# A table of steps for the output rows of one half batch: turns six steps later, ranks one step later

## The chip, the cores and the metric

The kernel runs on one core of one Trainium2 chip. The metric is the time of one execution on the device in microseconds (us), from the first to the last instruction with what lies around them. A core has engines that run at once and wait for each other through semaphores: TensorE (PE in the rows; PEld is its weight load), VectorE (DVE), ScalarE (ACT), GpSimd (POOL) and SyncE (SP), which here only issues DMA transfers.

## The reference

Three stages run one after another on 8 batches with 8 heads of 576 rows, 4608 rows of 512 numbers in all. Cut to what is computed:

```
a      = softmax(phi)                       # over 32 memory slots
k_m    = a^T k ;  v_m = a^T v               # per head, 32 x 64
x      = softmax(q k_m^T / 8) v_m           # attention over the slots
h      = x @ w_in                           # 512 -> 2048
g      = where(h > 0, h, exp(min(h, 0)) - 1)
y      = g @ w_out                          # 2048 -> 512
logits = y @ w_gate ;  e = argmax(logits)   # 8 experts
out    = softmax(logits)[e] * relu(y @ w1[e]) @ w2[e]
```

## The kernel before

**Units and steps.** The first two stages work on half batches: a batch b has two groups g of 288 rows. The hidden 2048 columns are cut into 16 pieces f, and a triple (b, g, f) is one unit. The list `seq` puts the units in order; the first batch is cut, so that pieces 0 to 7 of its group 1 come first, then all of its group 0 (units 8 to 23), then pieces 8 to 15 of group 1 (units 24 to 31). Units from 32 on are the second batch.

**What a step issues.** From unit 23 on, step i of the program first issues whatever was put on the list `bg` for it, then `mm1` of unit i+2 (six matmuls, L520), `elu` of it (ACT L527 and L528, DVE L529) and `split_g` of it (ACT L536, POOL L537), and last `mm2` of unit i (twelve matmuls, L551). Every engine takes its instructions in the order in which they are issued here: the kernel is written under a manual schedule, and nothing reorders them.

**What lies on the list.** For the batch after the one in hand, `attn_items` puts the pieces of its attention on steps 3 to 25 of a group: `a1` turns phi (DVE L347) and takes its maximum (L349), `a1e` is the exponential (ACT L356), `a2` turns the result back (PE L372, copied out by ACT L373), `a3` multiplies with k and v (PE L380), `a3b` scales and turns (DVE L390 to L399), `a4` makes the scores (PE L424, DVE L429), `a5` takes their maximum (DVE L434). `load_phi` (SP L201) fetches phi for the other half of the heads into the one buffer of its kind, once `a1` has read it. `a6n` folds v_m into w_in (PE L482, evacuated by ACT L491 and DVE L492) and then loads the next piece of w_in (SP L340). PE's small products share two PSUM buffers, `ps_m`.

**What follows a group.** When the last unit of a group is done, its sums stand in `ysb`, and `y_items` puts the rest on the steps behind it: the logits (`y_logit`, `y_logit2`), the ranks (`y_rank`: two matmul lines on PE, L611 and L612, and DVE L620 to L633), three scatters of row numbers (`y_scatter`, POOL L685), four turns of the sums into rows (`y_turn`, DVE L656, into the tile `yr`), the gate weights (`y_gate`, DVE L664 and L668), three multiplications by them (`y_times`, DVE L673), and the store of the rows to DRAM (`y_store`, SP L679, four DMAs of 144 KB). The tile `yr` has one buffer, so a group's first turn waits until the store of the group before it has landed.

For group 0 of the first batch the last step is 23, and its store stands at step 32; for group 1 the last step is 31, and what `y_items` puts for it counts from there. The steps are a table of thirteen numbers, `t`: logits, second logits, ranks, first scatter, four turns, two gate steps, three multiplications (the last of which is also the store's).

Of the kernel before, what the change touches and what calls it, by code (L numbers as in the profile page):

```python
# [57 lines left out]
def attn_moe_moe2_kernel(  # L58
# [112 lines left out]
    with ExitStack() as order:  # L171
        order.enter_context(tc.manual_schedule())
        setup()
        with ExitStack() as p1, ExitStack() as late_pool:
# [394 lines left out]
            def y_logit(b, g):  # L569
                ysb = st["y", b, g]  # L570
                ps = ps_m.tile([P, 512], F32, tag="m", name="ps_l")
                for c in range(NC):
                    nc.tensor.matmul(ps[32 * c:32 * c + 32, 0:G], wg[:, c, :], ysb[c], tile_position=(0, 32 * c))  # L573
                lp = l1.tile([P, G], F32, tag="e", name="lp", bufs=3)
                nc.scalar.copy(out=lp, in_=ps[:, 0:G])
                st["lp", b, g] = lp

            def y_logit2(b, g):
                lp = st.pop(("lp", b, g))
                ps = ps_m.tile([P, 512], F32, tag="m", name="ps_l2")  # L580
                n = G // PK
                for i in range(n):
                    nc.tensor.matmul(ps[:PK, E * i:E * i + E], lp[:, PK * i:PK * i + PK], sel)
                lg = ps[:PK, 0:n * E].rearrange("p (i e) -> p i e", e=E)
                tl = lambda shape, name, dt=F32: pool.tile(shape, dt, tag=name, name=name)
                bc = lambda x: x.to_broadcast([PK, n, E])
                mx = tl([PK, n, 1], "r_mx")
                nc.vector.tensor_reduce(out=mx, in_=lg, axis=AX.X, op=ALU.max)
                sh = tl([PK, n, E], "r_sh")
                nc.vector.tensor_tensor(out=sh, in0=lg, in1=bc(mx), op=ALU.subtract)  # L590
                ex = tl([PK, n, E], "r_ex")
                nc.scalar.activation(out=ex, in_=sh, func=AF.Exp)
                oh = tl([PK, n, E], "r_oh")
                nc.vector.scalar_tensor_tensor(
                    out=oh, in0=sh, scalar=0.0, in1=prio[:PK].unsqueeze(1).to_broadcast([PK, n, E]),
                    op0=ALU.is_ge, op1=ALU.mult,
                )
                nc.vector.tensor_reduce(out=mx, in_=oh, axis=AX.X, op=ALU.max)
                nc.vector.tensor_tensor(out=oh, in0=oh, in1=bc(mx), op=ALU.is_equal)
                gate = pool.tile([PK, n, 1], F32, tag="r_gate", name="r_gate", bufs=2)  # L600
                nc.vector.tensor_reduce(out=gate, in_=ex, axis=AX.X, op=ALU.add)
                nc.vector.tensor_scalar(out=gate, in0=gate, scalar1=1e-9, scalar2=None, op0=ALU.add)
                nc.vector.reciprocal(out=gate, in_=gate)
                st["oh", b, g], st["gate", b, g] = oh, gate

            def y_rank(b, g):
                oh = st.pop(("oh", b, g))
                n = G // PK
                flat_oh = oh.rearrange("p i e -> p (i e)")
                ps = ps_m.tile([P, 512], F32, tag="m", name="ps_r")  # L610
                nc.tensor.matmul(ps[:, 0:n * E], ones, flat_oh)  # L611
                nc.tensor.matmul(ps[:PK, 64:64 + n * E], tri, flat_oh)  # L612
                if b == 0 and g == 0:
                    nc.tensor.matmul(
                        ps[:, 128:128 + E], ident[0:PK, 0:1].to_broadcast([PK, P]), oh[:, 0, :]
                    )
                    nc.vector.tensor_copy(out=oh0, in_=ps[:, 128:128 + E])
                for i in range(n):
                    nxt = run[:, g, i + 1] if i + 1 < n else run[:, 1 - g, 0]
                    nc.vector.tensor_tensor(out=nxt, in0=run[:, g, i], in1=ps[:, E * i:E * i + E], op=ALU.add)  # L620
                rk = pool.tile([PK, n, E], F32, tag="r_sh", name="rk")
                nc.vector.tensor_tensor(
                    out=rk, in0=ps[:PK, 64:64 + n * E].rearrange("p (i e) -> p i e", e=E),
                    in1=run[:PK, g, 0:n], op=ALU.add,
                )
                nc.vector.tensor_tensor(out=rk, in0=rk, in1=oh, op=ALU.mult)
                df = pool.tile([PK, n, 1], F32, tag="r_mx", name="df")
                nc.vector.tensor_reduce(out=df, in_=rk, axis=AX.X, op=ALU.add)
                di = pool.tile([PK, n, 1], I32, tag="r_di", name="di", bufs=2)
                if (b, g) == (B - 1, 1):  # L630
                    st["df"] = df
                else:
                    nc.vector.tensor_copy(out=di, in_=df)  # L633
                st["di", b, g] = di
# [17 lines left out]
            def y_turn(b, g, c):  # L652
                if c == 0:
                    st["yr", b, g] = late["p"].tile([P, NB, NC, 32], F32, tag="yr", name="yr", bufs=1)
                x = st["y", b, g][c].rearrange("p (j s) -> p j s", s=32)
                nc.vector.transpose(out=st["yr", b, g][:, :, c], in_=x)  # L656

            def y_gate(b, g, part):
                gate = st["gate", b, g]
                k = PK // 32  # L660
                if part == 0:
                    g4 = st["g4", b, g] = pool.tile([P, G // PK, k], F32, tag="r_g4", name="r_g4")
                    for x in range(k):
                        nc.vector.tensor_copy(out=g4[0:32, :, x], in_=gate[32 * x:32 * x + 32, :, 0])  # L664
                else:
                    g4 = st["g4", b, g]
                    for x in range(1, 4):
                        nc.vector.tensor_copy(out=g4[32 * x:32 * x + 32], in_=g4[0:32])  # L668

            def y_times(b, g, i, n=NR):  # L670
                yr = st["yr", b, g].rearrange("p j c i -> p j (c i)")[:, n * i:n * i + n]
                g4 = st["g4", b, g].rearrange("p i x -> p (i x)")[:, n * i:n * i + n].unsqueeze(2)
                nc.vector.tensor_tensor(out=yr, in0=yr, in1=g4.to_broadcast([P, n, P]), op=ALU.mult)  # L673

            def y_store(b, g):
                yr = st["yr", b, g].rearrange("p j c i -> p j (c i)")
                rows = table[4 * S * b:4 * S * b + 4 * S, :].rearrange("(s j x) d -> x s j d", j=NJ, x=4)
                for x in range(4):
                    nc.sync.dma_start(out=rows[x, :, NB * g:NB * g + NB], in_=yr[32 * x:32 * x + 32])  # L679
# [3 lines left out]
            def y_scatter(b, g, i):  # L683
                t = (G // PK) * (2 * b + g) + i
                d = nc.gpsimd.indirect_dma_start(  # L685
                    out=itab.rearrange("a (l o) -> (a l) o", o=1),
                    out_offset=IndirectOffsetOnAxis(ap=st["di", b, g][:, i], axis=0),
                    in_=ids[:, t:t + 1], in_offset=None,
                )
                for x in scattered:  # L690
                    tc.declare_no_dep(d.ins, x.ins, reason="a token's place is its own")
                scattered.append(d)
# [80 lines left out]
            def y_items(b, g):  # L773
                t = [1, 2, 7, 8, 4, 4, 9, 9, 11, 13, 15, 16, 17] if g else [1, 2, 9, 10, 4, 5, 9, 11, 11, 12, 12, 13, 13]
                if b == 0 and g == 0:
                    t = [1, 2, 6, 7, 3, 4, 5, 5, 6, 6, 7, 8, 9]
                it = [
                    (t[0], lambda: y_logit(b, g)), (t[1], lambda: y_logit2(b, g)), (t[2], lambda: y_rank(b, g)),
                ]
                it += [(t[3] + i, lambda i=i: y_scatter(b, g, i)) for i in range(G // PK)]  # L780
                it += [(t[4 + c], lambda c=c: y_turn(b, g, c)) for c in range(NC)]
                it += [(t[8 + i], lambda i=i: y_gate(b, g, i)) for i in range(2)]
                it += [(t[10 + i], lambda i=i: y_times(b, g, i)) for i in range(NB // NR)]
                it += [(t[12], lambda: y_store(b, g))]
                if b == 0 and g == 0:
                    it += [(11, y_first)]
                return it
# [72 lines left out]
            for i, (b, g, f) in enumerate(seq):  # L860
# [20 lines left out]
                if f == NF - 1:  # L881
                    for s, fn in y_items(b, g):
                        at(i + s, fn)
# [524 lines left out]
```

## Time and profile before

| what | value |
|---|---|
| median of 3 runs | 1283.53 us (1281.06 to 1286.11) |
| the profiled execution's own time | 1290.46 us |
| its span, first to last instruction | 1288.7 us |
| PE busy | 1207.3 us, 94% of the span |
| DVE, ACT, POOL busy | 62%, 52%, 36% |
| mean granted clock of TensorE | 0.979 of full |
| the chain that ended last, by engine | PE 75%, DMA 8%, DVE 7% of the span |
| the store `table<-yr` in that chain | 1% of the span |

The profile is of one execution. It lists each instruction with its start from the beginning of the span, its duration, and how long its engine sat idle before it with the instruction or transfer that ended the idle time. "The chain that ended last" follows the work back from its last instruction, at each step to what released it. The granted clock is 1.00 at 2.4 GHz and 0.50 at 1.2 GHz.

### The profile page before, as it was taken

To read this page: it belongs to the slowest core of one execution; us is meant where nothing else is said; L and a number is where in the kernel's file an instruction comes from. 1 tells how busy PE (TensorE), PEld (TensorE's weight loads), DVE (VectorE), ACT (ScalarE), POOL (GpSimd) and SP (SyncE) were. 2 spreads that over 40 slices of the span, in tenths; PEclk is the share of its full clock that TensorE was granted. 3 is DMA by queue.
4 is the path that set the end of the run, shared out by engine and by line. 5 is a ranking of instruction groups with operands and counts; after the bars stand their busy time and mean duration, and the time that the engine had idled before them with its cause. 6 is when DMAs were issued, how large, how long until landed. Compare 5 with 4: busy or idle time off the path is not lost.

```text
span 1288.7 us, 26251 instructions
## 1 busy us (share of the span) xinstructions
PE 1207.3 (94%) x10026; PEld 1114.4 (86%) x10026; DVE 799.7 (62%) x1811; ACT 665.0 (52%) x1523; POOL 461.6 (36%) x497
## 2 busy tenths in 40 slices
PE   4488886999999999999999999999999999999997
PEld 2277766989989898899899899999999999999995
DVE  5899764655655564655656544673677666667672
ACT  3677543555555565555555555531445444445442
POOL 2656241353443443443444444412222321131102
PEclk9689998999999999999999999999999999999999
DMA  9776656643652544544451252314578777557763
GB/s 232 195 211 193 180 114 125 123 110 77 126 125 51 132 118 55 150 94 93 121 91 42 85 168 57 74 21 121 137 185 259 212 205 241 156 144 194 215 209 95
DMA packets 113786, 178.41 MB, mean 138 GB/s; under 512 B 10745, under 2 KB 79609, under 8 KB 110064
## 3 DMA queue, kind: packets, MB, share of 16 engines
q1 hardware_dynamic: 105632, 157.09, 47.9%
q0 software_dynamic: 8016, 19.52, 5.4%
q8 instruction: 82, 1.34, 0.5%
q14 instruction: 56, 0.46, 0.2%
HBM read 171.62 MB, written 42.76 MB: 166 GB/s over the span
## 4 chain that ended last, share of the span: by engine, by line
PE 75%; DMA 8%; DVE 7%; issue 4%; ACT 3%; POOL 1%; SPq 1%; POOLq 0%; DVEq 0%; ACTq 0%
PE ps_acc L551 27%; PE ps_h L520 15%; PE ps_h L1081 14%; PE ps_acc L1096 12%; DMA kv<-in_v_dram 3%; PE ps_M L482 2%; PE ps_kv L380 2%; DMA out_dram<-xr,idw 1%; DMA table<-yr 1%; PE ps_s L424 1%; DMA win_x<-in_moe_w_in_dram 1%; PE ps_l L573 1%; DVE e L529 1%; PE ps_a L372 1%; DVE gl L537 1%
## 5 line engine op out<-in xcount | busy, mean ns | idle before, releaser
L537 POOL TENSOR_TENSOR gl<-e,gh 128x288 fp32r<-128x288 f32 x237 | 196.3, 828 | 394.0 <-ACT gh L536 306.9
L520 PE MATMUL ps_h<-ath,wt 128*128 128x288 f32 x1024 | 262.6, 313 | 9.2 <-DVE e L529 8.3
L529 DVE SCALAR_TENSOR_TENSOR e<-e,ps_h 128x288 f32<-128x288 f32 x256 | 114.1, 446 | 207.0 <-ACT e L528 189.1
L520 PEld LDWEIGHTS ps_h<-ath,wt 128*128 128x128 f32 x1024 | 182.0, 192 | 54.0 <-issue 30.0
L536 ACT CAST gh<-e 128x288 fp32r<-128x288 f32 x256 | 110.4, 432 | 185.4 <-DVE e L529 183.6
L551 PE MATMUL ps_acc<-gh,wt 128*128 128x288 f32 x1024 | 179.3, 297 | 3.4 <-ACT gh L536 3.3
L551 PE MATMUL ps_acc<-gl,wt 128*128 128x288 f32 x1024 | 178.4, 296 | 1.6 <-DVE gl L537 1.6
L551 PE MATMUL ps_acc<-gh,wl 128*128 128x288 f32 x1024 | 178.3, 296 | 0.0
L1084 ACT ACTIVATE hh<-ps_h 128x288 fp32r<-128x288 f32 x128 | 52.6, 411 | 225.7 <-PE ps_h L1081 200.9
L1081 PE MATMUL ps_h<-xh,wt 128*128 128x288 f32 x1024 | 164.8, 300 | 2.2 <-ACT xh L747 1.0
L551 PEld LDWEIGHTS ps_acc<-gh,wt 128*128 128x128 f32 x1024 | 151.3, 190 | 4.7 <-ACT gh L536 4.5
L520 PE MATMUL ps_h<-atl,wt 128*128 128x288 f32 x512 | 152.8, 298 | 0.5 <-POOL atl L470 0.5
L551 PEld LDWEIGHTS ps_acc<-gl,wt 128*128 128x128 f32 x1024 | 151.1, 189 | 2.3 <-DVE gl L537 2.3
L1081 PEld LDWEIGHTS ps_h<-xh,wt 128*128 128x128 f32 x1024 | 144.7, 189 | 8.9 <-ACT xh L747 5.5
L551 PEld LDWEIGHTS ps_acc<-gh,wl 128*128 128x128 f32 x1024 | 150.7, 190 | 0.0
L527 ACT ACTIVATE e<-ps_h 128x288 f32<-128x288 f32 x256 | 104.6, 409 | 59.7 <-PE ps_h L520 49.9
L1085 DVE SCALAR_TENSOR_TENSOR hl<-ps_h,hh 128x288 fp32r<-128x288 f32 x128 | 58.2, 455 | 121.2 <-ACT hh L1084 113.6
L1109 POOL DMA_INDIRECT out_dram<-xr,idw x42 | 42.7, 1016 | 240.3 <-DMA xr<-od 215.7
L528 ACT ACTIVATE e<-e 128x288 f32<-128x288 f32 x256 | 113.9, 445 | 8.1
L520 PEld LDWEIGHTS ps_h<-atl,wt 128*128 128x128 f32 x512 | 99.1, 193 | 0.7 <-POOL atl L470 0.7
L1096 PE MATMUL ps_acc<-hh,wl 128*128 128x288 f32 x576 | 90.8, 299 | 1.3 <-issue 1.3
L1081 PE MATMUL ps_h<-xl,wt 128*128 128x288 f32 x512 | 89.5, 296 | 1.3 <-DVE xl L748 1.3
(214 smaller groups left out, 1924.2 us busy)
## 6 DMA issues: line engine op xcount, KB each, us to landing
raw<-in_moe_w_dram SPq DMA_DIRECT2D x30, 2048.0 KB
win<-win_s SPq DMA_DIRECT2D x28, 1024.0 KB
xd<-xr SPq DMA_DIRECT2D x17, 576.0 KB
xg<-xd SPq DMA_DIRECT2D x68, 144.0 KB
kv<-in_k_dram SPq DMA_DIRECT2D x16, 576.0 KB
kv<-in_v_dram SPq DMA_DIRECT2D x16, 576.0 KB
table<-yr SPq DMA_DIRECT2D x64, 144.0 KB
od<-ot SPq DMA_DIRECT2D x64, 144.0 KB
```

The source lines that it names most:

```text
L520: nc.tensor.matmul(ps, x[:, u, fo:fo + P], y[:, u], start=(n == 0), stop=(n == 3 * NQ - 1))
L527: nc.scalar.activation(out=e, in_=ps, func=AF.Relu, scale=-1.0)
L528: nc.scalar.activation(out=e, in_=e, func=AF.Exp, scale=-1.0)
L529: nc.vector.scalar_tensor_tensor(out=e, in0=e, scalar=-1.0, in1=ps, op0=ALU.add, op1=ALU.max)
L536: nc.scalar.copy(out=gh, in_=e)
L537: eng.tensor_tensor(out=gl, in0=e, in1=gh.bitcast(F32), op=ALU.subtract)
L551: nc.tensor.matmul(acc[c], x[:, f, P * c:P * c + P], y, start=(first and n == 0), stop=(final and n == 2),)
L1081: nc.tensor.matmul(ps, w1_at(p, y, c, f), x[:, c], start=(n == 0), stop=(n == 3 * NC - 1))
L1084: nc.scalar.activation(out=h, in_=ps, func=AF.Relu)
L1085: V.scalar_tensor_tensor(out=l, in0=ps, scalar=0.0, in1=h.bitcast(F32), op0=ALU.max, op1=ALU.subtract)
L1096: nc.tensor.matmul(acc[c], w2t[p][:, y, f, P * c:P * c + P], x, start=(f + n == 0), stop=(f == NF2 - 1 and n == 2),)
L1109: d = nc.gpsimd.indirect_dma_start(out=out, out_offset=IndirectOffsetOnAxis(ap=at(n), axis=0), in_=xp["r"][:, n], in_offset=None, bounds_c ...
```

## The change

One table of steps is split off for group 1 of the first batch. Until now that group used the table of all groups 1.

```diff
                 t = [1, 2, 7, 8, 4, 4, 9, 9, 11, 13, 15, 16, 17] if g else [1, 2, 9, 10, 4, 5, 9, 11, 11, 12, 12, 13, 13]
                 if b == 0 and g == 0:
                     t = [1, 2, 6, 7, 3, 4, 5, 5, 6, 6, 7, 8, 9]
+                elif b == 0:
+                    t = [1, 2, 8, 9, 10, 10, 12, 12, 11, 13, 15, 16, 17]
```

The turns go from steps 35, 35, 40, 40 to 41, 41, 43, 43; the ranks from 38 to 39; the scatters, which count from the fourth number, from 39 to 41 to 40 to 42. Gates, multiplications and store stay.

On DVE at step 35, behind the last vector work of step 34, stand the turns (`yr`) and the turn of phi (`pT`) with its maximum (`nm`):

```order
 L648 SCALAR_TENSOR_TENSOR rowb<-erow,less 128x8 [waits DVE_49]
 L529 SCALAR_TENSOR_TENSOR e<-e,ps_h 128x288 [waits Activation_49]
-L656 STREAM_TRANSPOSE yr<-ysb 128x9x32 [waits DMAHW2_49,DMAHW7_49,DMAHW1_49,DMAHW0_49]
-L656 STREAM_TRANSPOSE yr<-ysb 128x9x32
-L347 STREAM_TRANSPOSE pT<-phi_t 128x576
+L347 STREAM_TRANSPOSE pT<-phi_t 128x576 [waits DMAHW7_49]
 L349 TENSOR_REDUCE nm<-pT 128x1 [waits DVE_49]
```

The first two turns, with their wait for the four DMAs of a store, no longer stand ahead of phi's turn, which has a DMA wait of its own instead.

On PE at steps 38 and 39 stand the products for w_in (`ps_M`), the ranks (`ps_r`), matmuls of units, and `a3` (`ps_kv`):

```order
 L482 MATMUL ps_M<-win,vT 32x512 x8
-L611 MATMUL ps_r<-r_oh,ones 128x24
-L612 MATMUL ps_r<-r_oh,tri 96x24
 L520 MATMUL ps_h<-ath,wt_82 128x288
...
 L551 MATMUL ps_acc_1951<-gl,wt_82 128x288
+L611 MATMUL ps_r<-r_oh,ones 128x24
+L612 MATMUL ps_r<-r_oh,tri 96x24
 L380 MATMUL ps_kv<-kv,a 32x128 x24
```

The two rank matmuls move from directly behind `ps_M` to directly ahead of `ps_kv`, past the 18 matmuls of a step.

On DVE at steps 40 to 43, behind `a3b`, stand the vector part of the units (`e`), the gates (`r_g`), the scores (`sT`) and their maximum (`mx`):

```order
 L399 STREAM_TRANSPOSE kT<-kvm 32x64 x4
-L529 SCALAR_TENSOR_TENSOR e<-e,ps_h 128x288 x2
-L664 COPY r_g_2364<-r_gate 32x3 x3
+L529 SCALAR_TENSOR_TENSOR e<-e,ps_h 128x288
+L656 STREAM_TRANSPOSE yr<-ysb 128x9x32 x2
+L529 SCALAR_TENSOR_TENSOR e<-e,ps_h 128x288
+L664 COPY r_g_2362<-r_gate 32x3 x3
 L429 STREAM_TRANSPOSE sT<-ps_s 128x288 x2
 L529 SCALAR_TENSOR_TENSOR e<-e,ps_h 128x288
+L656 STREAM_TRANSPOSE yr<-ysb 128x9x32 x2
 L434 TENSOR_REDUCE mx<-sT 128x18
```

One pair of turns now stands between the vector work of two units at step 41, the other ahead of the scores' maximum at step 43.

## Rows read from the trace of the kernel before

**Rows 1.** Chain that ended last, 180 to 220 us: start, us, what.
```profile
189.18 15.80 DMA table<-yr
205.17 0.84 DVE yr L656 x2
206.01 0.67 DVE pT L347
208.62 1.52 PE ps_a L372 x6
```

**Rows 2.** Waits on PE, 180 to 260 us: total, times, longest.
```profile
PE ps_a L372 <- ACT aT L356: 8.6, 1, 8.6
PE ps_r L611 <- DVE wt L492: 1.5, 1, 1.5
```

**Rows 3.** Timeline of PE: start, us, instruction, [idle before, releaser].
```profile
199.31 0.69 PE L551 MATMUL ps_acc<-gl,wt 128*128 128x288 f32 x4
...
213.81 1.09 PE L482 MATMUL ps_M<-win,vT 64*32 64x512 f32 x16
216.36 0.40 PE L611 MATMUL ps_r<-r_oh,ones 96*128 96x24 f32 x2 [1.46 <-DVE wt L492]
...
216.77 0.38 PE L520 MATMUL ps_h<-ath,wt 128*128 128x288 f32 x1
...
219.34 1.52 PE L380 MATMUL ps_kv<-kv,a 96*32 96x128 f32 x48
...
225.67 0.82 PE L372 MATMUL ps_a<-ident,aT 128*96 128x128 f32 x6
226.25 0.38 PE L520 MATMUL ps_h<-ath,wt 128*128 128x288 f32 x1
...
228.81 1.20 PE L424 MATMUL ps_s<-big,kT 32*32 32x288 f32 x32
...
238.88 0.29 PE L520 MATMUL ps_h<-ath,wt 128*128 128x288 f32 x1
```

**Rows 4.** Windows: stretch, engines' busy us, granted clock, DMA share, GB/s.
```profile
198.00:200.00 2.00, 2.00 (x16) 1.77 (x14) 0.00 (x0) 0.00 (x0) 0.02 (x1) 1.00 1.05 79
204.00:206.00 2.00, 0.00 (x0) 0.00 (x0) 0.83 (x3) 0.00 (x0) 0.00 (x0) 0.50 0.73 279
210.00:212.00 2.00, 2.00 (x9) 2.00 (x9) 0.75 (x2) 1.38 (x4) 0.81 (x1) 0.50 0.00 0
214.00:216.00 2.00, 0.90 (x16) 0.00 (x0) 0.66 (x2) 1.44 (x3) 0.79 (x1) 1.00 0.01 4
```

**Rows 5.** Timeline of ACT, the steps that follow phi's turn.
```profile
207.49 1.06 ACT L356 ACTIVATE aT<-pT,nm 128x576 f32<-128x576 f32 x1 [10.41 <-DVE nm L349]
...
212.08 0.85 ACT L373 COPY a<-ps_a 96x384 f32<-96x384 f32 x2
```

**Rows 6.** Timeline of DVE, 196 to 237 us.
```profile
196.16 0.45 DVE L529 SCALAR_TENSOR_TENSOR e<-e,ps_h 128x288 f32<-128x288 f32 x1
...
209.44 0.45 DVE L529 SCALAR_TENSOR_TENSOR e<-e,ps_h 128x288 f32<-128x288 f32 x1 [1.99 <-ACT e L528]
...
216.97 0.55 DVE L620 TENSOR_TENSOR run<-run,ps_r 128x8 f32<-128x8 f32 x3
...
218.06 0.17 DVE L633 CAST di<-df 96x3 int32<-96x3 f32 x1
...
219.27 0.77 DVE L347 STREAM_TRANSPOSE pT<-phi_t 128x576 f32<-128x576 f32 x1
...
222.94 0.45 DVE L529 SCALAR_TENSOR_TENSOR e<-e,ps_h 128x288 f32<-128x288 f32 x1 [2.12 <-ACT e L528]
...
228.78 0.46 DVE L529 SCALAR_TENSOR_TENSOR e<-e,ps_h 128x288 f32<-128x288 f32 x1 [2.10 <-ACT e L528]
...
236.89 0.46 DVE L529 SCALAR_TENSOR_TENSOR e<-e,ps_h 128x288 f32<-128x288 f32 x1 [3.40 <-ACT e L528]
```

**Rows 7.** Timeline of SP, the DMAs that it issues.
```profile
184.09 0.34 SPq L340 DMA_DIRECT2D win<-win_s  x1
187.29 2.85 SPq L679 DMA_DIRECT2D table<-yr  x4
192.76 0.34 SPq L340 DMA_DIRECT2D win<-win_s  x1
206.70 0.35 SPq L201 DMA_DIRECT2D phi_t<-in_phi_dram  x1
```

## Prediction

> **What bounds the kernel now.** I read the page first: PE is busy for 94% of the span, and most of the chain that ended last is its matmuls. So only an edit that takes an idle stretch off PE, or adds one, moves the time. Then the waits on PE around the place of the change. From 180 to 260 us there are two of size [rows 2]: 8.6 us before the first `a2` of the second half's work (step 37), and 1.5 us before the ranks (step 38).
>
> The chain says where the 8.6 us come from [rows 1]. The store of group 0's rows takes 15.80 us from its last issue to its landing; only then can DVE begin the turns of group 1 (205.17), which write the same buffer; behind them stand phi's turn (206.01), its maximum, the exponential on ACT (207.49 [rows 5]) and at last PE's `a2` (208.62). DVE had been ready since its vector work of 196.16 plus 0.45 us [rows 6]. The reader is to see that phi's turn needs nothing from that store. It stands behind the turns on an engine that works in order.
>
> The windows show a second price [rows 4]: the granted clock is 1.00 while PE still works (198 to 200 us), 0.50 in the idle stretch and also from 210 to 212 us, when PE is busy again, and 1.00 from 214 us. That is 1.2 GHz in place of 2.4 GHz for the first matmuls after the idle stretch.
>
> **The change part by part.** Times are those of the profiled execution.
>
> The turns out of step 35. Phi's turn can start at 196.61. From there to the exponential is what it was: 207.49 less 206.01, 1.48 us, so ACT starts at 198.09, 9.40 us earlier than before. `a2` came 1.13 us after that start (208.62 less 207.49), so it could begin at 199.22. PE is free at 200.00 (208.62 less 8.62; the last group before it started at 199.31 [rows 3]). So the exponential is ready 0.8 us before PE, and the whole 8.62 us goes.
>
> The clock. From `a2` to the next `ps_M` took 5.19 us at half clock (208.62 to 213.81). The same row of work, six transposes, `mm1` and `mm2`, took 3.14 us later at full clock (225.67 to 228.81 [rows 3]). Without the idle stretch nothing lowers the clock: 2.05 us gained.
>
> What is late next. The chain of ACT and DVE behind the exponential keeps its own pace, shifted by 9.40 us. The unit's vector work of 209.44 ends at 200.49, and `mm1` behind `a2` wants that buffer at 200.58: no wait. The copies of `a2` (212.08, 0.85 us [rows 5]) end at 203.53, and `ps_M` needs the buffers that they free; PE would be there at 200.00 + 3.14 = 203.14. A new wait of 0.39 us.
>
> The ranks. PE waited 1.46 us for the evacuation of `ps_M` [rows 3], since the two small buffers were both taken. Now `mm1` of step 38 follows `ps_M` at once, and the ranks come 18 matmuls later. Those took 2.57 us (216.77 to 219.34), more than the 1.46 us for which the evacuation was late, so it is done by then: 1.46 us gained. Their own 0.41 us on PE (216.36 to 216.77) moves and stays. On DVE they take 1.26 us (216.97 to 218.23), and that now stands ahead of the second phi turn of step 39. The vector work behind it, which ended at 223.39, would end 1.26 us later against PE, and its buffer is wanted at 226.25: 1.6 us of cover are left, so nothing. The scatters go one step later with them on POOL; nothing on PE waits for a scatter.
>
> The turns at their new steps. A pair is 0.84 us. At step 40 a pair goes from ahead of `a3b`, so DVE is 0.8 us sooner there. At step 41 the pair stands where DVE sat idle for 2.10 us waiting for ACT (228.78 [rows 6]); at step 43 ahead of `mx`, where the next unit's vector work had waited 3.40 us for ACT's exponential and ended at 237.35, 1.5 us before the matmul that needs its buffer (238.88). Full delay of 0.84 us is covered. The wait for the store itself: 205 us against about 216 for step 41. Cost nothing; if all cover were gone, 0.84 us for each pair.
>
> Phi's second load. SP issued it at 206.70, at the end of phi's turn, into an idle queue, and no DMA moved after 210 us [rows 4, 7]: at most 3.3 us. Now it is issued at about 197.3, with the store and the load of `win` (192.76) still under way; they keep the DMAs busy until about 206. If it goes behind them, it lands between 206 and 206 + 3.3 = 209.3. It is wanted at 219.27 - 11.74 + 1.26 = 208.8, and PE feels it only after the 1.6 us of cover, from 210.4 on. I take zero, with a loss of up to 4.9 us kept for the range (worked out below). By the Trainium skill (DMA: Bandwidth & Descriptors, "Queues, rings and completion order") each DMA engine takes a queue's descriptors in ring order, which puts this load behind the whole store. The store's landing at 205 and the burst of 279 GB/s that ends by 206 [rows 1, 4] agree with one after another. By that rule the landing is the later one above; with bandwidth shared out, the sooner one; the sum is the same by both.
>
> Sum: 8.62 + 2.05 + 1.46 - 0.39 = 11.74 us. The steps after the place keep their order and their distances, so the gain stays to the end. The profiled execution, 1290.46 us of its own (span 1288.7 us), would be 1278.7; the median of the runs shown, 1283.53, goes to 1271.8.
>
> Bounds: at most 8.62 + 2.05 + 1.46 = 12.1 us if no new wait appears. The other end is set by the rivals.
>
> **The rivals.**
> *Phi's load takes the store's place.* For it: it now enters the queue in a stretch that moved only 79 GB/s at full DMA share [rows 4], and the store took 15.80 us there. Against it: by 204 to 206 us the DMAs moved 279 GB/s again. If a second slow stretch as long as from 198 to 204, 6 us, struck this load, it would land at 209.3 + 6 = 215.3; DVE's second phi turn would wait, and PE would lose 215.3 - 210.4 = 4.9 us. Gain 6.8 us, 1276.7. The ring order that the Trainium skill states (DMA: Bandwidth & Descriptors, "Queues, rings and completion order") is what would put the load into this place.
>
> *The wait is mostly the profiled execution's own.* It took 6.93 us more than the median. If all of that lay in this one wait, plain runs would lose only 8.62 - 6.93 = 1.69 us there, and no clock. The gain is then 1.69 + 1.46 - 0.39 = 2.8 us: 1280.8. Against it: in the page's chain DMAs hold 8% of the span and this store 1%, so a surplus of slow DMAs would lie mostly elsewhere.
>
> *The change does not do what it says.* In the new order phi's turn waits on a DMA semaphore (DMAHW7) that is one of the four for which the turns waited. If that meant the store's second part, the stall would remain and only 1.46 us would go: 1282. Against it: these count up, and phi's first load was issued on it before the store, as its own transfer, so its count is reached long before.
>
> *Slower.* One mechanism: DVE stuck at step 39 on phi's second load for longer than it was at step 35 on the store. Place: the second phi turn; price: each us of landing after 210.4 is a us on PE, with the clock's 2.05 us once it idles long. Break-even is a landing at about 220, slower by 0.5% (6.4 us) at about 226, which is 29 us after issue, where the longest transfer here took 15.80 us. At 230 it would be 1293. Only a queue blocked twice over does that.
>
> **How the numbers follow.** Forecast 1271.8 us at 0.74; phi's load late, 1276.7, at 0.10; the profile's own wait, 1280.8, at 0.11; not as it says, 1282, at 0.02; slower, 1293, at 0.03. The forecast's own range is 1268.5 to 1275: 12.1 us of gain and the runs' spread of 2.5 us below and above the median. For 8 in 10 I go up into the second and third case, to 1279. What a measurement of this kernel can tell from no change is 0.5%, 6.4 us, so faster means under 1277.1: nearly all of the first case (0.73), half of the second (0.05), a fifth of the third (0.02), 0.80 together. Within it 0.17, slower 0.03.
>
> **What would show it.** In the changed profile PE's wait before `a2` at about 200 us is under 1 us, and the granted clock stays at 1.00 from 196 to 216 us; `ps_kv` of step 39 starts near 207.6 in place of 219.34; DVE's turns at about 216 and 220 wait for no DMA; the ranks do not appear among PE's waits. Wrong would be: a wait for phi's load at DVE's second phi turn that reaches PE, a wait for `e` (L529) on PE's `mm1` at steps 43 to 47 above 1 us, or a group of waits elsewhere that has grown by what was won here.

## The result and the profile after

The changed kernel takes 1271.85 us (median of 4 runs, 1269.79 to 1273.14); before, on the same chip, takes 1282.57 us. The ratio is 0.9911, with a 95% interval of 0.9885 to 0.9937. Once more with more rounds it was 1272.22 us beside 1283.77 us, ratio 0.9911 (0.9898 to 0.9924). The forecast was 1271.8 us.

The profiled spans differ by more, 1288.7 to 1271.4 us, and the place of the change does not hold all of that: a second profile of before (below) has a span of 1284.1 us with the same stall in it, so the first one was slow elsewhere too. So I read the place by itself, from the `ps_M` of step 34 to the `ps_kv` of step 39, in both timelines of PE.

The timeline of PE after, the stretch that answers to [rows 3] (start, us, instruction, idle before where there was a wait):

```profile
193.52 1.09 PE L482 MATMUL ps_M<-win,vT 64*32 64x512 f32 x16
...
201.82 0.82 PE L372 MATMUL ps_a<-ident,aT 128*96 128x128 f32 x6
...
205.23 1.46 PE L482 MATMUL ps_M<-win,vT 64*32 64x512 f32 x16
206.62 0.40 PE L520 MATMUL ps_h<-ath,wt 128*128 128x288 f32 x1
...
209.13 0.30 PE L611 MATMUL ps_r<-r_oh,ones 96*128 96x24 f32 x2
...
209.53 1.52 PE L380 MATMUL ps_kv<-kv,a 96*32 96x128 f32 x48
```

No row has an idle time. From 193.52 to 209.53 are 16.01 us. Before, the same stretch began with this row of PE's timeline:

```profile
191.54 1.09 PE L482 MATMUL ps_M<-win,vT 64*32 64x512 f32 x16
```

It ended at 219.34 [rows 3], after 27.80 us: 11.79 us won at the place.

All waits on PE from 180 to 260 us, to be set beside [rows 2]:

```profile
PE ps_acc L551 <- ACT gh L536: 0.6, 1, 0.6
PE ps_h L520 <- POOL atl L470: 0.5, 1, 0.5
PE ps_l L573 <- DVE wt L492: 0.5, 1, 0.5
```

Both waits of before are gone, and none of their size has come. The windows (stretch, engines' busy us, granted clock, DMA share, GB/s), as [rows 4]:

```profile
200.00:202.00 2.00, 2.00 (x17) 2.00 (x17) 0.06 (x1) 1.84 (x4) 0.00 (x0) 1.00 1.27 94
206.00:208.00 2.00, 2.00 (x25) 1.38 (x11) 0.58 (x2) 1.41 (x4) 0.57 (x1) 1.00 0.76 275
214.00:216.00 2.00, 2.00 (x18) 1.99 (x17) 0.92 (x4) 1.38 (x6) 0.07 (x1) 1.00 1.10 234
```

The DMAs are as slow as before (94 GB/s at full share), but PE works through that time, and the clock stays at 1.00. On DVE the turns stand where they were put, and phi's second turn has no wait for its load. DVE's timeline after:

```profile
198.51 0.77 DVE L347 STREAM_TRANSPOSE pT<-phi_t 128x576 f32<-128x576 f32 x1
...
209.63 0.56 DVE L620 TENSOR_TENSOR run<-run,ps_r 128x8 f32<-128x8 f32 x3
...
210.31 0.75 DVE L626 TENSOR_TENSOR rk<-rk,r_oh 96x24 f32<-96x24 f32 x1
...
211.38 0.77 DVE L347 STREAM_TRANSPOSE pT<-phi_t 128x576 f32<-128x576 f32 x1
...
214.94 0.45 DVE L529 SCALAR_TENSOR_TENSOR e<-e,ps_h 128x288 f32<-128x288 f32 x1 [2.00 <-ACT e L528]
...
217.86 0.83 DVE L656 STREAM_TRANSPOSE yr<-ysb 128x288 f32<-128x288 f32 x2
...
223.12 0.83 DVE L656 STREAM_TRANSPOSE yr<-ysb 128x288 f32<-128x288 f32 x2
```

### The profile page after: what moved, and what is told of

Read it like the earlier page. It is cut to its first block, busy times and chain, and to the rows that moved or that the text cites. A ratio compares the mean times of both kernels' runs of the same rounds, so it can differ in the third digit from the quotient of the medians.

```text
span 1271.4 us, 26251 instructions
## 1 busy us (share of the span) xinstructions
PE 1202.2 (95%) x10026; PEld 1110.1 (87%) x10026; DVE 799.4 (63%) x1811; ACT 663.2 (52%) x1523; POOL 461.1 (36%) x497
## 4 chain that ended last, share of the span: by engine, by line
PE 74%; DVE 8%; DMA 7%; issue 4%; ACT 3%; POOL 2%; SPq 1%; POOLq 0%; DVEq 0%; ACTq 0%
PE ps_acc L551 28%; PE ps_h L520 15%; PE ps_h L1083 12%; PE ps_acc L1098 10%; PE ps_M L482 3%; PE ps_kv L380 2%; DMA out_dram<-xr,idw 1%; PE ps_s L424 1%; DVE e L529 1%; DMA kv<-in_v_dram 1%; DMA big<-in_q_dram 1%; DMA xg<-xd 1%; PE ps_l L573 1%; DVE gl L537 1%; DMA win_x<-in_moe_w_in_dram 1%
## 5 line engine op out<-in xcount | busy, mean ns | idle before, releaser
L520 PE MATMUL ps_h<-ath,wt 128*128 128x288 f32 x1024 | 261.0, 311 | 10.7 <-DVE e L529 9.8
```

What stands on the lines that cost most here:

```text
L520: nc.tensor.matmul(ps, x[:, u, fo:fo + P], y[:, u], start=(n == 0), stop=(n == 3 * NQ - 1))
```

## The experiments

My theory: the gain is the wait for the store (8.6 us) with the half clock behind it, and the wait before the ranks; nothing else moved. Rivals: the ranks carry it, DVE's order is a cost in itself, the stall belongs to one execution, or phi's load has little or no cover. The place is told by three distances in PE's timeline: from the `ps_M` of step 34 to `a2`, from there to the `ps_M` of step 38, from there to `ps_kv`.

| kernel | to `a2` | to `ps_M` | to `ps_kv` | together | ratio of time to before (95%) |
|---|---|---|---|---|---|
| before | 17.08 | 5.19 | 5.53 | 27.80 | |
| before again | 16.43 | 5.56 | 5.52 | 27.51 | |
| after | 8.30 | 3.41 | 4.30 | 16.01 | 0.9911 (0.9885 to 0.9937) |
| after again | 8.29 | 3.41 | 4.30 | 16.00 | 0.9911 (0.9898 to 0.9924) |
| turns only | 8.29 | 3.41 | 6.36 | 18.06 | 0.9932 (0.9910 to 0.9955) |
| ranks only | 16.45 | 5.20 | 3.92 | 25.57 | 0.9992 (0.9974 to 1.0011) |
| own buffer | 8.44 | 3.97 | 7.56 | 19.97 | 0.9952 (0.9934 to 0.9970) |
| own buffer, ranks later | 8.47 | 3.98 | 4.29 | 16.74 | 0.9929 (0.9917 to 0.9942) |
| turns one step later | 8.30 | 7.69 | 8.88 | 24.87 | 0.9989 (0.9976 to 1.0002) |
| filler | 17.05 | 3.98 | 7.90 | 28.93 | 1.0060 (1.0033 to 1.0087) |
| ranks later, filler in two buffers | 16.23 | 3.98 | 4.28 | 24.49 | 1.0045 (1.0029 to 1.0062) |
| phi four times | 8.30 | 3.41 | 4.29 | 16.00 | 0.9983 (0.9968 to 0.9997) |
| scatters late | 8.45 | 3.97 | 6.38 | 18.80 | 0.9970 (0.9952 to 0.9988) |

**The two halves of the change.** Each half alone, as a difference to the changed kernel:

```diff
-                    t = [1, 2, 8, 9, 10, 10, 12, 12, 11, 13, 15, 16, 17]
+                    t = [1, 2, 7, 8, 10, 10, 12, 12, 11, 13, 15, 16, 17]
```

> Only the turns stand six steps later; ranks and scatters stay. Theory: the gain is the store's wait and the clock, so PE's wait before a2 (8.6 us) and the half clock (2.05 us) go, less 0.4 us of a new wait, 10.3 us in all: about 1272.3 us beside 1282.6, and PE's wait of 1.5 us before the ranks stays in the profile. Rival (the ranks carry the gain): within 3 us of before.

```diff
-                    t = [1, 2, 8, 9, 10, 10, 12, 12, 11, 13, 15, 16, 17]
+                    t = [1, 2, 8, 9, 4, 4, 9, 9, 11, 13, 15, 16, 17]
```

> Only the ranks (and their scatters) stand one step later; the turns stay. Theory: PE's wait before the ranks (1.5 us) goes, the 8.6 us before a2 and the half clock stay: 1.5 us faster, about 1281, hardly to be told from before by time, but to be seen in the waits. Rival (the ranks carry the gain): 10 us faster.

The turns alone give 0.9932, 1274.08 us beside 1283.92, and 9.7 us at the place; the ranks alone 0.9992, and 2.2 us at the place, of which 0.6 us are a shorter stall in that execution and 1.6 us the distance from `ps_M` to `ps_kv` (5.53 to 3.92). The rival falls. The rows of PE's timeline with the turns alone, and the window behind them (columns as above), show the ranks' wait a little larger than before, and no fall of the clock after it:

```profile
202.46 1.46 PE L482 MATMUL ps_M<-win,vT 64*32 64x512 f32 x16
205.85 0.40 PE L611 MATMUL ps_r<-r_oh,ones 96*128 96x24 f32 x2 [1.93 <-DVE wt L492]
```

```profile
206.00:208.00 2.00, 2.00 (x17) 2.00 (x18) 1.49 (x8) 0.57 (x2) 0.00 (x0) 1.00 1.02 414
```

**Another buffer in place of other steps.** Before's steps, with a pool of its own for this group's rows, open from the end of the first stage until the expert weights need the room:

```diff
-                    st["yr", b, g] = late["p"].tile([P, NB, NC, 32], F32, tag="yr", name="yr", bufs=1)
+                    yp = late["x"] if (b, g) == (0, 1) else late["p"]
+                    st["yr", b, g] = yp.tile([P, NB, NC, 32], F32, tag="yr", name="yr", bufs=1)
...
+                late["x"] = extra.enter_context(tc.tile_pool(name="extra", bufs=1, reuse_waits="tile"))
...
```

> Before's steps, but the group's rows are turned into a buffer of their own, so no turn waits for the store. Theory (the wait for the store is all, and the place matters only through it): the 8.6 us and the 2.05 us go; the pair of turns, 0.84 us, stays ahead of phi's turn and the ranks' 1.5 us stays, so 9.4 us faster, about 1273. Rival (DVE's order itself is the cost, or the DMAs hold phi or w_in too): less than 3 us faster, or a wait for another DMA appears in place of it.

`a2` comes on time with the turns still ahead of phi's turn: the wait for the buffer was the cost, not the place. But only 7.8 us are won where 9.4 were expected. The row of PE's timeline with the ranks' wait, then the windows (columns as above), show why: the clock falls behind that wait.

```profile
207.05 0.40 PE L611 MATMUL ps_r<-r_oh,ones 96*128 96x24 f32 x2 [1.93 <-DVE wt L492]
```

```profile
206.00:208.00 2.00, 0.95 (x8) 0.95 (x9) 1.59 (x4) 0.76 (x2) 0.66 (x1) 1.00 0.97 321
208.00:210.00 2.00, 2.00 (x12) 2.00 (x12) 1.18 (x8) 0.86 (x2) 0.00 (x0) 0.63 0.62 254
210.00:212.00 2.00, 2.00 (x22) 1.67 (x24) 1.50 (x3) 0.87 (x2) 1.25 (x2) 0.52 0.01 4
```

So I ran it with the ranks one step later as well (the new buffer, and `t = [1, 2, 8, 9, 4, 4, 9, 9, 11, 13, 15, 16, 17]`):

> The buffer of its own for that group's rows (turns at their old steps, no wait for the store) with the ranks one step later. Theory: with the store's wait gone the ranks' wait has grown to 1.9 us and, with the buffer alone, the clock fell behind it; without it the clock stays at 1.00 and the step of a3 comes some 3 us sooner than with the buffer alone, 10.9 us sooner than before: about 1273. Rival (the clock fell for another reason): the same dip to about 0.5 shows, and the time stays at 1277.

`ps_kv` came 3.2 us sooner than with the buffer alone and 11.1 us sooner than before; the time was 1274.78 us beside 1283.77. The windows show no dip:

```profile
208.00:210.00 2.00, 2.00 (x49) 1.97 (x52) 1.84 (x7) 0.89 (x3) 0.41 (x1) 1.00 0.94 386
210.00:212.00 2.00, 2.00 (x28) 1.80 (x21) 1.90 (x5) 0.00 (x0) 0.40 (x1) 1.00 0.41 109
```

So the ranks' wait of 1.9 us can cost 3 us in all. It does not always: with the turns alone the same 1.93 us passed without a dip, and so it did with the scatters late (below), where PE's idle times at the place are the same as here. What decides is open.

**How far the turns have to go.** The first pair one step later only, as a difference to the changed kernel:

```diff
-                    t = [1, 2, 8, 9, 10, 10, 12, 12, 11, 13, 15, 16, 17]
+                    t = [1, 2, 7, 8, 5, 5, 9, 9, 11, 13, 15, 16, 17]
```

> The turns of the first pair stand one step later than before (36 in place of 35), behind phi's turn but still ahead of the store's landing; ranks as before. Theory: DVE still waits for the store until about 205 us of before's profile, now with the vector work of the next unit behind it; a2 starts on time, the copies of a2 on ACT come late, and PE waits some 4.7 us before the w_in products of step 38; no half clock if that wait is short. Gain 8.62 + 2.05 - 4.7 = 6 us, about 1276.6. Rival (any place behind phi's turn will do): 10 us faster, as with all six steps.

The wait moved as expected, from `a2` to `ps_M`, and PE's idle time was 4.3 us where 4.7 were expected. The condition "no half clock" was wrong, as PE's timeline and then the windows show:

```profile
207.73 2.33 PE L482 MATMUL ps_M<-win,vT 64*32 64x512 f32 x16 [4.27 <-ACT a L373]
```

```profile
206.00:208.00 2.00, 0.27 (x1) 0.18 (x2) 2.00 (x4) 1.13 (x4) 0.62 (x1) 0.50 0.48 185
212.00:214.00 2.00, 2.00 (x10) 2.00 (x11) 1.13 (x8) 0.00 (x0) 0.00 (x0) 0.50 1.00 422
```

From `ps_M` to `ps_kv` the stretch takes 8.88 us, nearly all of it at half clock and 1.4 us of it the ranks' wait. Of the 6 us expected 2.9 stay at the place, and the time, 1281.99 us, can't be told from before. So the rival that any place behind phi's turn will do falls: one step is far too few. Between one step and six nothing was run.

**The clock by itself.** Before, with 60 matmuls of fill ahead of that `a2`; then the same with the ranks moved and the fill in two buffers (its edit is shown, without that of the ranks):

```diff
+            def filler(b):
+                for _ in range(2 if b == 2 else 0):
+                    ps = ps_m.tile([P, 512], F32, tag="m", name="ps_f")
+                    for _ in range(30):
+                        nc.tensor.matmul(ps[:, 0:G], identr, wl[:, 0, 0:G], start=True, stop=True)
...
-                    (5, lambda: a2(b, 0)),
+                    (5, lambda: (filler(b), a2(b, 0))),
```

> Before, with 60 matmuls of 128x288 whose result nobody reads put ahead of that a2, so that PE works through the wait for the store. Theory (2.05 us of the gain are TensorE's clock): a2 still starts when the exponential is done, the granted clock stays at 1.00 from 196 to 216 us, and the six transposes with mm1 and mm2 take 3.1 us in place of 5.2: about 2 us faster than before, 1280.6. Rival (the clock is no separate term, the work behind a2 is held by ACT and DVE): no faster, the stretch from a2 to the w_in products still 4 us or more.

> The kernel with only the ranks moved (the turns and the wait for the store stay), with 60 matmuls of 128x288 whose result nobody reads ahead of that a2, this time into two buffers, so that the two small PSUM buffers alternate afterwards as they did. Theory (the clock's 2.05 us is in part cover: behind the exponential ACT and DVE need some 4 us anyway before the w_in products can start): from a2 to those products 4.0 us in place of 5.2, clock 1.00 throughout, about 1.2 us faster than with the ranks alone, 1281 to 1283, and nothing lost later. Rival (the loss with the first filler came from the extra matmuls themselves): some 9 us slower than before again.

At the place both did what the second text says: 3.98 us from `a2` to `ps_M` at a clock of 1.00, where half clock takes 5.2; the 3.1 us of the first text did not come. PE's timeline with two filler buffers, and a window behind it:

```profile
209.08 0.86 PE L372 MATMUL ps_a<-ident,aT 128*96 128x128 f32 x6
...
213.06 1.46 PE L482 MATMUL ps_M<-win,vT 64*32 64x512 f32 x16
```

```profile
210.00:212.00 2.00, 1.59 (x12) 1.60 (x13) 0.65 (x2) 1.19 (x3) 0.81 (x1) 1.00 0.00 0
```

So 1.2 us of the 2.05 us are the clock's alone; the other 0.8 us are in any case the pace of ACT and DVE, if `a2` starts as late as the exponential. But in time both lost, 0.6% and 0.45%, where both texts expected a gain. With one filler buffer part of that is at the place: the ranks waited 1.9 us, and the clock fell there (0.59 and 0.55 in the windows from 216 to 220 us). With two, the place gained 1.1 us beside the ranks alone, and in the two profiled executions some 6 us were lost later, bit by bit from about 415 us on. PE's waits of `ps_kv` for the load of v are 10.2 us over the whole run, against 8.1 with the ranks alone, which is a part of it at most. That the loss is due to the extra matmuls themselves was the rival, and it stands; by what way is open.

**Phi's load late on purpose.** After, with that one load issued four times:

```diff
-                nc.sync.dma_start(out=t, in_=phi[b, 4 * u:4 * u + 4].rearrange("h (s j) m -> (h s) (j m)", j=NJ))
+                for _ in range(4 if (b, u) == (2, 1) else 1):
+                    nc.sync.dma_start(out=t, in_=phi[b, 4 * u:4 * u + 4].rearrange("h (s j) m -> (h s) (j m)", j=NJ))
```

> After, with phi's second load of that half batch issued four times in a row, each after the one before has landed, so that it lands late on purpose. Theory (PE has 1.6 us of cover behind DVE's second phi turn, then pays each us): landing at about 217 us in after's profile, where the turn stood at 211.4, some 5.6 us late, costs 4 us on PE, perhaps 2 more if the clock falls: 1275.9 to 1278. Rival (PE has far more cover): as fast as after, 1271.9. Rival (all of DVE's wait is PE's): 5.6 us and more, 1277.5 up.

The four took longer than thought, and DVE waited 9.4 us in place of 5.6. The waits on DVE, then PE's timeline, then the first two of the four loads in the chain that ended last (the lines of this kernel are numbered one higher):

```profile
DVE pT L348 <- DMA phi_t<-in_phi_dram: 9.4, 1, 9.4
```

```profile
220.49 0.88 PE L373 MATMUL ps_a<-ident,aT 128*96 128x128 f32 x3 [7.26 <-ACT aT L357]
222.53 0.87 PE L373 MATMUL ps_a<-ident,aT 128*96 128x128 f32 x3 [1.17 <-DVE kvm L393]
```

```profile
196.22 12.71 DMA phi_t<-in_phi_dram
208.94 3.21 DMA phi_t<-in_phi_dram
```

PE's first wait is 2.1 us shorter than DVE's, so there is cover, and the rival that all of DVE's wait is PE's falls, though the time, 1282.66 us, lies where that rival put it. It is another cover than the one in the prediction: `a2` waits here for the exponential, while the prediction's 1.6 us belong to `mm1` behind it, which waits for the vector work. With the second wait and the half clock, from `ps_kv` of step 39 to that of step 43 it took 25.21 us (206.43 to 231.64) where after takes 13.38: 11.8 us, the whole gain, and the time was 0.9983 of before. So the mechanism of phi's load coming late is real and its price, with the clock, higher than I put it.

The first of the four loads is the one that the changed kernel makes too. Behind the store and a load of `win` it took 12.71 us, against 3.21 us for the next one, which was issued when the DMAs were nearly idle (a share of 0.09 in the window from 208 to 210 us). It landed at 208.93. DVE had been free for it since 208.39, 9.36 us ahead of the turn at 217.75. So the changed kernel is near the edge: a load that comes one or two us later would be felt on PE.

**What makes the store slow.** Before, with the three scatters of group 0 moved behind the store:

```diff
-                    t = [1, 2, 6, 7, 3, 4, 5, 5, 6, 6, 7, 8, 9]
+                    t = [1, 2, 6, 13, 3, 4, 5, 5, 6, 6, 7, 8, 9]
```

> Before, with the three scatters of row numbers of the first group (POOL, 4 bytes for each row) moved from steps 30 to 32 to steps 36 to 38, behind the store; turns and ranks as before. Theory A (the scatters slow the DMAs for some us, and with them the store): the store lands before 197 us, the turns no longer wait, and the kernel is 9.4 us faster, about 1273. Theory B (the two loads of w_in pieces, 1 MB each, around the store hold it): the store lands as late as before, within 2 us, and the time stays within 3 us of before.

Theory A holds at the place: the turns at 198.23 no longer wait, with turns and buffer as before, and the place is 9.0 us shorter. Its time was missed, 1280.51 us in place of 1273. PE waits 3.86 us for the load of v at step 43, with half clock behind it (48 matmuls in 2.79 us in place of 1.52). The scatters, now at 204.50 to 208.83 us, have the next group's three right behind them, and the load stands among those: it took 15.02 us, against 11.67 us in the kernel with its own buffer, where the first three scatters were issued by 188.01. That fits the same slowing, though only this one run shows it. A row of DVE's timeline and two of PE's, then the load of v in the chain, first here, then with the own buffer:

```profile
198.23 0.83 DVE L656 STREAM_TRANSPOSE yr<-ysb 128x288 f32<-128x288 f32 x2
```

```profile
209.06 0.40 PE L611 MATMUL ps_r<-r_oh,ones 96*128 96x24 f32 x2 [1.93 <-DVE wt L492]
...
229.17 2.79 PE L380 MATMUL ps_kv<-kv,a 96*32 96x128 f32 x48 [3.86 <-DMA kv<-in_v_dram]
```

```profile
214.01 15.02 DMA kv<-in_v_dram
```

```profile
213.51 11.67 DMA kv<-in_v_dram
```

The ranks' wait is 1.93 us here too, and the window behind it shows no dip:

```profile
210.00:212.00 2.00, 2.00 (x16) 1.89 (x15) 1.19 (x8) 0.85 (x2) 0.00 (x0) 1.00 0.77 45
```

**Before once more**, unchanged:

> Before once more, for a second profile of it. The first profiled execution took 1290.5 us, 7.9 us over the median. Theory: that surplus lies elsewhere, so this one again shows PE waiting 8 to 9 us before a2 of step 37 and 1.5 us before the ranks, at a time of 1281 to 1286 us. Rival (the long wait belongs to that one execution): a wait of 1 to 4 us.

It took 1285.87 us, and the waits on PE are the same two:

```profile
PE ps_a L372 <- ACT aT L356: 8.0, 1, 8.0
PE ps_r L611 <- DVE wt L492: 1.5, 1, 1.5
```

The rival that the stall was mostly one execution's own falls.

**The change once more:**

> The changed kernel once more, with more rounds, beside the two above. Theory: 11 to 12 us won at the place of the change and nothing given back later, so a ratio to before of 0.991, and again no wait on PE of over 1 us from 196 to 230 us. Rival (part of the gain is given back later, or belongs to single executions): a ratio of 0.994 or more.

The place is the same to 0.01 us, and the ratio too. No version that I ran is faster.

## Why the prediction was right

**The wait for the store** was put at 8.62 us. From `ps_M` of step 34 to `a2` it is 17.08 before and 8.30 after: 8.78 us. The turns alone and the buffer alone both take it away; the ranks alone leave it.

**The clock and what is late next** were put at 2.05 - 0.39 = 1.66 us. From `a2` to `ps_M` it is 5.19 to 3.41: 1.78 us. The new wait shows in `ps_M` itself, 1.39 us from its start to the next matmul (205.23 to 206.62) in place of some 1.0. The fillers say how the term is made up: 1.2 us by the clock alone, the rest only because the exponential is early.

**The ranks** were put at 1.46 us. The last stretch gave 5.53 - 4.30 = 1.23 us, since `ps_M`'s own wait lies in it; alone, 1.61 us. What the prediction did not see is that this wait would have been 1.9 us, once the store's is gone, and could bring the clock down: moving the ranks is worth 2.1 us beside the turns and 3.2 us beside the buffer.

**Sum:** 11.74 us forecast, 11.79 us measured at the place. The gain stays up to the last `a3` of the kernel: that `ps_kv` starts at 684.41 after and at 696.03 in the second profile of before. The median of the runs moved by 10.7 us and, in the second comparison, by 11.6 us. That the forecast time came out to a twentieth of a us is luck: the terms are off by up to 0.2 us in both directions, the median of before moved by 1 us with one more run, and the interval of the ratio is some 3 us wide to each side. By its own terms (1283.53 less 12.1 less 2.5) the forecast's range begins at 1268.9, not 1268.5; nothing hangs on it.

**The signs** came. `ps_kv` of step 39 starts at 209.53 and was put at 207.6; the stretch begins 1.98 us later in the profile after (193.52 against 191.54), which is the difference.

**The moved pieces at no cost** held. The turns wait for no DMA at 217.86 and 223.12, and PE shows no wait for the vector work behind them. The ranks cost DVE 1.85 us (209.63 to 211.48) where 1.26 were expected, because one of their instructions took 0.75 us. The cover was enough, but thinner than the 1.6 us in the prediction: the vector work behind phi's second turn ends at 215.39, 1.06 us before the matmul that needs its buffer (216.45 in PE's timeline):

```profile
216.45 0.38 PE L520 MATMUL ps_h<-ath,wt 128*128 128x288 f32 x1
```

Phi's second load was at no cost by a small margin. In the changed kernel it came in time for 211.38, 12.1 us after its issue; in the kernel that issues it four times the first took 12.71 us. That is the later of the prediction's two landings (209.3 less 197.3, 12.0 us after the issue), and a little more.

**The rivals.** Phi's load late: did not happen in two profiles of the changed kernel, but was shown to be real by force. The profile's own wait: fell. Not as it says: fell, phi's turn began at 198.51 with no wait. Slower: nothing of it.

## What to carry to other kernels

On an engine that works in order, look at what stands behind a wait: here two turns of half a microsecond, in no hurry themselves, held up for 8.6 us a chain that PE needed. The cure can be the place or a second buffer. The place costs no memory, but it has to lie behind the landing of the awaited transfer: here one step later only moved the wait. Price a PE wait with the matmuls that follow it at half clock, and ask first what else would pace them: with `a2` as late as before, a full clock gave back 1.2 of the 2.05 us.

## What the runs showed of the hardware

Small scatters slowed the transfers after them. With three scatters of 96 numbers of 4 bytes each ahead of it, the store of 576 KB, first issued at 187.29 [rows 7], landed at 204.98 (189.18 plus 15.80 [rows 1]), 17.7 us later. Without them it was first issued at 189.00 and had landed by 198.23, since the turns began there without a wait: 9.2 us at most. The row of SP's timeline with the scatters late:

```profile
189.00 2.03 SPq L679 DMA_DIRECT2D table<-yr  x4
```

Moved, they came with a wait of 3.9 us for another load, as shown above.

The DVE instruction of 0.75 us (`rk`, 0.18 us in before's timeline) has two inputs in SBUF, and it ended at 211.06, just when POOL's subtraction beside it did (210.22 plus 0.81 us, POOL's timeline after):

```profile
210.22 0.81 POOL L537 TENSOR_TENSOR gl<-e,gh 128x288 fp32r<-128x288 f32 x1 [1.98 <-ACT gh L536]
```

The Trainium skill (SBUF — State Buffer, "SBUF: two separate sides") says that VectorE and GpSimd share a pair of ports which one instruction holds to its end, against a DVE operation with two SBUF inputs too. The trace agrees here, and with the ranks alone too: there POOL's subtraction ends at 219.07 and `rk`, which begins later beside it, takes 0.33 us and ends at 219.11.

An idle time of 4.3 us on PE was followed by half clock. One of 1.93 us was followed by a fall of the clock in two kernels (own buffer, filler) and not in two others (turns alone, scatters late), so its length alone does not decide.
